# The second and third block of an attention and feed-forward kernel: GpSimd's transfers add half of each group of keys and values, VectorE sums the other half, and the order of all instructions is another

## The chip, the cores and the metric

The kernel runs on one core of one Trainium2 chip. The metric is the device time of one execution in microseconds (us). The core's engines run side by side, each through a queue of its own: TensorE (PE in the views; PEld are its loads of weights), VectorE (DVE), ScalarE (ACT), GpSimd (POOL) and SyncE (SP), which here only issues transfers. A transfer (DMA) is issued by an engine's queue (SPq, POOLq) and done by 16 DMA engines.

## The reference

Two parts, one after the other. Attention over 8 batches and 8 heads, 576 tokens, 64 numbers for each head, in which keys and values are first averaged over groups of eight tokens, so that 576 keys become 72. Then a gated layer over the 4608 tokens with 512 inputs and 1536 hidden numbers.

```python
k_p = k.reshape(B, H, Sp, pool, D).mean(axis=3)      # pool = 8, Sp = 72
v_p = v.reshape(B, H, Sp, pool, D).mean(axis=3)
scores = scale * np.matmul(q, k_p.transpose(0, 1, 3, 2))
scores = scores - np.max(scores, axis=-1, keepdims=True)
attn = np.exp(scores)
attn = attn / (np.sum(attn, axis=-1, keepdims=True) + 1e-09)
return np.matmul(attn, v_p).astype(np.float32)
...
gate = 1.0 / (1.0 + np.exp(-(x @ w_gate)))
val = x @ w_val
return (gate * val @ w_out).astype(np.float32)
```

## The kernel before

The tokens are cut into nine blocks of 512. Block 0 goes alone through the layer, the other eight go in pairs, with sums and differences of blocks and weights that save products. Every large matrix is used as a high and a low half, so a product is three matmuls. The function `first_pass` does attention for blocks 0 to 2 and the whole layer for block 0; after it `attention` does two pairs of heads of a block at a time, beside the products of the pair ahead (`hidden`, `second_sums`).

The host lays keys out as `kT` (for each batch and pair of heads 128 rows, 64 numbers of two heads, by 576 tokens) and values as `vm` (128 rows, the first 64 groups of two heads, by 64 numbers of eight tokens each) and `vr` (the last eight groups). The eight tokens of a group are neighbours, so the sum over a group is a reduction of VectorE over the last axis. `fill` (lines 621 to 637) issues the transfer of a tile and returns this view of it, `pool` (640) sums it. In `first_pass`, `load_k` (1200), `load_v` (1206) and `load_r` (1209) fill tiles for blocks 1 and 2: eight tiles of keys (128x576) and eight of values (128x512), and `keys` (1218) and `v_sum` sum them. For block 0 the keys come the same way, one whole tile for each pair of heads (`h<-in_kT` in the trace), and its values are summed by TensorE from plain rows (`vn`) and a matrix of ones (`sums8`): these are the matmuls `vr` and `vp`. The constants (`const`, tile `cst`: a unit matrix and masks) come in one transfer of 68.5 KB. Sums of keys are put into `kbd`, tiles with two heads on the diagonal, which GpSimd sets to zero first; scores are `sc`. `place_vres` and `v_put` write the values of the last groups into `vres` by a mask, one half for each head.

Some matmuls of the first pass have no reader: `bank_for` issues as many as the table `UNREAD` says ahead of a product, on `kbd` or on the unit matrix in `cst`, into the tile that the product then fills. They appear as `sc<-kbd`, `tr<-cst`, `tp<-cst` and `av<-cst`.

What sets the order: `first_pass` reads the word list `ORDER`, and each word records one step; `Book` takes down every instruction as a unit and nothing is issued. At the end all units are issued in the order of the table `LATER`, 3717 numbers that were found by search. Each engine keeps to its part of that order, and waits in it are for data and for buffers.

Of the kernel before, what the change touches and what calls it, by code (L numbers as in the profile page):

```python
# [19 lines left out]
P = 128  # L20
# [103 lines left out]
6 20 18 9 19 2 26 16 101 25 14 35 21 86 7 24 87 11 29 36 34 0 5 37 4 46 41 27 47 45 88 3 32 31 42 15 30 38 13 75 28 39  # L124
17 83 44 93 56 77 10 57 68 43 52 53 12 23 50 58 78 48 79 54 94 33 61 51 84 81 67 65 59 22 89 82 95 40 102 66 128 74 72
99 73 71 117 64 163 1 132 96 164 124 165 131 137 130 166 126 100 138 134 60 97 151 177 139 62 98 111 121 85 112 135 113
185 114 127 136 152 184 153 122 129 154 125 157 145 173 133 160 182 146 183 156 147 168 123 209 188 192 55 238 148 144
69 149 142 140 141 155 143 76 103 161 159 243 80 104 105 189 116 271 106 187 107 190 191 150 115 108 176 109 201 170
110 202 200 216 171 217 215 167 180 218 169 193 213 158 220 211 197 224 212 225 198 194 70 195 242 174 199 229 344 227
226 205 233 175 208 222 210 206 203 228 204 223 221 277 172 234 214 240 232 181 196 241 207 252 255 235 236 219 260 262  # L130
268 237 256 239 231 265 251 247 162 263 254 253 280 267 279 275 230 304 286 283 289 310 266 257 278 290 269 294 313 272
246 282 179 285 296 245 291 178 287 258 90 288 321 284 322 327 350 292 264 328 281 331 270 332 347 369 244 333 348 312
298 259 346 345 340 302 316 261 91 354 274 276 376 293 305 378 297 309 299 361 92 315 352 355 303 364 250 301 356 320
391 119 365 329 372 366 338 317 379 306 359 308 307 384 383 393 49 395 311 349 439 318 353 362 462 403 324 314 397 339
373 249 408 375 343 351 494 273 248 374 367 326 440 396 394 387 436 385 386 382 368 388 498 370 407 377 447 399 337 406
450 390 454 295 341 458 334 502 319 445 444 118 423 420 342 424 323 425 421 360 507 381 380 466 491 409 449 520 389 410
524 457 435 120 499 426 467 357 468 413 481 427 418 422 485 463 541 433 464 414 434 465 459 441 442 496 484 412 497 438
506 428 508 469 483 510 411 415 448 511 455 475 417 501 523 392 477 443 482 504 489 540 490 542 480 500 509 437 429 543
503 486 532 470 471 460 566 430 431 476 472 473 517 474 495 512 492 300 514 416 515 527 567 522 529 568 521 461 531 325
533 583 576 330 526 516 571 493 537 335 519 525 528 589 544 577 518 534 546 581 586 535 585 539 556 557 595 538 358 548  # L140
553 604 363 608 559 545 530 536 582 550 547 609 551 371 569 560 549 554 570 606 336 555 579 400 627 432 610 561 633 580
634 563 552 565 624 614 564 628 562 404 635 611 629 186 625 588 587 596 584 640 617 603 618 591 638 592 605 575 590 639
572 626 574 558 573 630 724 631 632 594 578 642 647 601 593 649 613 612 615 452 664 730 600 678 620 619 675 607 679 637
621 667 622 676 623 641 598 672 636 668 673 644 597 680 513 479 648 674 398 599 669 488 654 646 689 655 677 401 446 704
602 643 670 671 453 662 698 653 699 657 487 700 659 616 661 731 684 650 683 658 701 666 451 702 660 697 707 713 708 686
709 688 744 703 681 705 687 706 685 694 682 695 651 690 726 725 732 656 711 733 728 691 710 719 717 1034 712 743 692
718 785 714 645 723 746 693 663 720 456 715 665 721 696 716 478 722 749 754 751 736 735 741 734 739 769 738 737 740 770
727 745 747 748 1033 764 753 755 729 774 768 761 756 765 419 779 767 772 742 809 777 807 759 758 757 793 760 773 778
776 780 781 782 783 771 752 784 402 787 775 766 797 811 791 798 801 1035 803 799 1082 806 786 1037 405 788 813 789 804
814 790 850 825 1036 802 652 826 851 822 817 810 853 794 855 827 1263 805 859 856 808 819 1083 818 820 834 843 812 816  # L150
815 831 823 848 844 832 833 824 840 828 841 795 837 838 63 881 821 864 829 894 830 862 912 852 839 871 842 915 792 860
849 865 835 908 872 878 836 916 877 918 882 868 880 869 866 800 867 909 874 879 910 870 899 873 845 900 926 875 846 901
876 911 896 897 941 898 905 902 927 942 854 928 913 903 904 943 906 914 907 886 885 936 1038 847 994 505 884 998 887
930 1039 931 1081 888 932 917 929 861 1040 937 1043 950 893 933 934 1042 935 949 925 892 956 921 923 938 890 957 1084
958 883 1041 891 940 953 922 924 954 939 889 955 1063 895 1265 951 967 1264 1138 944 1064 863 1268 945 1266 1136 1066
1267 963 1137 959 948 962 977 1272 750 974 978 1269 1068 960 965 979 966 952 1271 971 946 857 972 920 1065 973 1067 975
976 1273 1085 1086 988 964 1146 999 968 1344 995 1008 983 1087 1274 1009 996 1089 763 1000 1091 1088 1270 961 997 1090
980 1018 981 1111 1054 1275 1112 1055 1019 1113 1116 1115 982 1010 1002 947 1114 1139 1056 1003 1140 1011 1141 1012 987
1004 1013 8 1147 1016 1014 986 1119 1212 1030 796 1050 1051 990 969 984 1015 1346 993 1345 919 1020 1120 985 1211 1069
1183 1121 1024 762 858 970 989 1347 1025 1348 1026 1131 1017 1132 1021 1353 991 1031 1148 1022 1349 992 1070 1133 1032  # L160
1023 1073 1350 1060 1074 1354 1351 1005 1213 1027 1416 1098 1352 1075 1006 1356 1142 1134 1044 1355 1052 1007 1099 1150
1047 1053 1135 1057 1149 1061 1058 1071 1028 1072 1059 1076 1045 1077 1048 1143 1102 1095 1046 1100 1247 1078 1214 1152
1049 1535 1144 1096 1092 1106 1001 1101 1029 1062 1122 1107 1108 1418 1145 1079 1117 1123 1109 1169 1417 1154 1103 1421
1128 1118 1151 1422 1124 1104 1423 1170 1164 1419 1420 1093 1425 1080 1166 1094 1215 1216 1153 1097 1171 1129 1167 1165
1110 1184 1158 1172 1185 1125 1426 1193 1161 1159 1427 1187 1246 1162 1130 1174 1428 1189 1188 1488 1160 1155 1424 1248
1191 1176 1186 1194 1228 1217 1192 1156 1175 1126 1536 1202 1127 1157 1195 1163 1205 1179 1173 1177 1220 1168 1537 1222
1221 1203 1178 1219 1218 1190 1105 1249 1206 1230 1208 1196 1180 1209 1316 1236 1231 1223 1315 1204 1181 1317 1197 1250
1224 1244 1489 1238 1325 1490 1198 1229 1237 1210 1234 1257 1235 1239 1233 1232 1207 1241 1276 1182 1260 1245 1258 1493
1199 1242 1251 1491 1243 1492 1200 1277 1240 1295 1318 1278 1252 1259 1261 1300 1319 1225 1320 1326 1335 1254 1226 1253
1400 1296 1494 1285 1289 1329 1336 1496 1255 1256 1399 1227 1302 1538 1495 1279 1337 1292 1333 1327 1301 1293 1280 1384  # L170
1290 1294 1281 1282 1283 1303 1262 1284 1201 1357 1297 1497 1304 1334 1305 1298 1498 1328 1572 1299 1321 1360 1306 1286
1291 1307 1287 1378 1361 1338 1310 1385 1308 1389 1311 1401 1331 1380 1379 1312 1451 1394 1358 1404 1499 1313 1339 1397
1500 1314 1405 1370 1391 1395 1340 1322 1390 1461 1396 1323 1288 1366 1309 1363 1403 1359 1448 1574 1364 1573 1429 1406
1575 1402 1407 1381 1408 1462 1362 1410 1409 1398 1324 1330 1577 1432 1392 1341 1332 1449 1433 1438 1342 1382 1393 1434
1515 1452 1377 1479 1365 1516 1411 1576 1442 1430 1412 1413 1578 1581 1501 1371 1580 1376 1463 1414 1450 1443 1445 1477
1517 1415 1431 1446 1372 1466 1478 1447 1439 1444 1373 1582 1539 1454 1467 1480 1584 1374 1649 1502 1504 1579 1540 1375
1583 1481 1383 1533 1505 1437 1440 1343 1518 1544 1435 1436 1464 1603 1519 1468 1525 1441 1455 1545 1546 1465 1367 1482
1456 1566 1503 1534 1453 1520 1459 1469 1457 1552 1549 1547 1460 1458 1470 1368 1483 1585 1507 1369 1484 1550 1601 1548
1650 1591 1551 1652 1508 1471 1567 1602 1386 1509 1472 1387 1526 1473 1476 1632 1553 1506 1604 1475 1474 1586 1595 1653
# [183 lines left out]
def attention_then_ffn(ctx: ExitStack, tc: tile.TileContext, qT, kT, vm, vr, vn, sums8, wgv, wo, const, out, outT):  # L363
# [253 lines left out]
    def slot(b, p):  # L617
        return (b * PAIRS + p) % RING


    def fill(raw, kind, *at):
        if kind == "k":
            nc.sync.dma_start(raw, kT[at])
            return raw.rearrange("p (g t) -> p g t", t=POOL)
# [512 lines left out]
    def first_pass():  # L1137
# [62 lines left out]
        def load_k(j, p):  # L1200
            raws["k", j, p] = fill(raw_room(), "k", j, p)
# [344 lines left out]
```

## Time and profile before

| | |
|---|---|
| median of 3 runs | 876.58 us (876.39 to 876.77) |
| the profiled execution | 876.07 us |
| its span, from first to last instruction | 874.2 us |
| TensorE busy | 865.1 us, 99% of the span |
| TensorE weight loads | 755.9 us, 86% |
| VectorE busy | 684.5 us, 78% |
| ScalarE busy | 540.6 us, 62% |
| GpSimd busy | 24.3 us, 3% |
| granted TensorE clock, mean | 0.999 |
| transfers | 223.11 MB, 255 GB/s over the span |

An engine is busy while it executes an instruction; issuing transfers and waiting are not busy. Times in the views are counted from the start of the span, so the execution's time is the span and some 1.9 us around it.

### The profile page before, as it was taken

The numbers are of one execution on the slowest core, as the hardware profiler recorded it, in microseconds if no ns is written. First come the engines' busy times: TensorE is split into PE (matmuls) and PEld (weight loads), VectorE is DVE, ScalarE is ACT, GpSimd is POOL, SyncE is SP. The second block draws the span as 40 slices with busy tenths as digits, with TensorE's granted clock in tenths as the row PEclk, the third lists the DMA queues.
The fourth block names the chain that finished last, engine by engine and source line by source line (L and its number), as shares of the span: only waits on it lengthen the run. The fifth ranks groups of instructions, "written<-read, shape, count | busy, mean of one in ns | idle before, by whom it ended". The sixth has DMA issues, their size and how long they took to land.

```text
span 874.2 us, 12442 instructions
## 1 busy us (share of the span) xinstructions
PE 865.1 (99%) x4327; PEld 755.9 (86%) x4327; DVE 684.5 (78%) x1067; ACT 540.6 (62%) x981; POOL 24.3 (3%) x60
## 2 busy tenths in 40 slices
PE   8999999999999999999999999999999999999997
PEld 8788888888888888888888888888888888888886
DVE  7999999999999999766779996455588945443973
ACT  7999897688888566565465647433456542233442
POOL 1000000021201000000000000000000000000000
PEclk9999999999999999999999999999999999999999
DMA  9999978999968797787856787666536765766466
GB/s 348 377 334 351 352 255 314 311 339 326 349 254 290 254 318 254 235 278 266 258 198 199 238 293 247 225 205 204 170 119 225 245 195 200 264 199 190 133 206 190
DMA packets 97277, 223.11 MB, mean 255 GB/s; under 512 B 10304, under 2 KB 29248, under 8 KB 95680
## 3 DMA queue, kind: packets, MB, share of 16 engines
q1 hardware_dynamic: 92096, 203.98, 69.3%
q0 software_dynamic: 5120, 18.35, 5.4%
q8 instruction: 34, 0.56, 0.3%
q14 instruction: 27, 0.22, 0.1%
HBM read 168.81 MB, written 53.48 MB: 254 GB/s over the span
## 4 chain that ended last, share of the span: by engine, by line
PE 96%; DMA 1%; DVE 1%; ACT 1%; issue 0%; SPq 0%; DVEq 0%; ACTq 0%
PE chain L333 56%; PE acc L333 28%; PE av L333 4%; PE sc L333 4%; PE tp L333 2%; DMA xs<-in_vn 1%; DMA h<-in_kT 0%; PE vp L333 0%; DVE y L333 0%; PE tr L333 0%; DVE zs L333 0%; ACT L333 0%; SPq L333 0%; DVE h L333 0%; ACT e L333 0%
## 5 line engine op out<-in xcount | busy, mean ns | idle before, releaser
L333 PE MATMUL chain<-xo,parts 128*128 128x512 f32 x2316 | 517.5, 381 | 0.1
L333 PEld LDWEIGHTS chain<-xo,parts 128*128 128x128 f32 x2316 | 433.7, 189 | 61.6 <-DVE y L333 0.7
L333 PE MATMUL acc<-hs,oparts 128*128 128x512 f32 (+1 forms) x1011 | 224.2, 380 | 0.0
L333 PEld LDWEIGHTS acc<-hs,oparts 128*128 128x128 f32 x1011 | 189.3, 189 | 26.4 <-issue 0.2
L333 DVE TENSOR_TENSOR y<-chain,sV 128x512 f32<-128x512 f32 x69 | 46.7, 685 | 49.9 <-PE chain L333 29.6
L333 DVE TENSOR_TENSOR y<-chain,sG 128x512 f32<-128x512 f32 x69 | 46.9, 686 | 43.0 <-PE chain L333 31.1
L333 ACT COPY sG<-chain 128x512 f32<-128x512 f32 x69 | 39.8, 585 | 60.9 <-PE chain L333 60.9
L333 DVE TENSOR_TENSOR hs<-h,hs 128x1024 fp32r<-128x1024 f32 x52 | 63.0, 1219 | 11.5 <-ACT hs L333 11.5
L333 ACT CAST hs<-h 128x1024 fp32r<-128x1024 f32 x52 | 54.5, 1050 | 26.9 <-PE acc L333 26.5
L333 ACT COPY sV<-chain 128x512 f32<-128x512 f32 x69 | 39.8, 584 | 39.4 <-PE chain L333 33.3
L333 ACT ACTIVATE gate<-y 128x512 f32<-128x512 f32 x69 | 43.2, 630 | 32.8 <-DVE y L333 24.4
L333 ACT CAST hs<-s 128x1024 fp32r<-128x1024 f32 x36 | 37.6, 1048 | 30.4 <-DVE s L333 11.8
L333 ACT ACT_TABLE_LOAD x39 | 50.0, 1283 | 3.2 <-DVE y L333 2.6
L333 DVE TENSOR_TENSOR h<-y,gate 128x512 f32<-128x512 f32 x69 | 46.9, 687 | 1.0
L333 DVE TENSOR_TENSOR hs<-s,hs 128x1024 fp32r<-128x1024 f32 x36 | 43.7, 1218 | 4.8 <-ACT hs L333 4.5
L333 PE MATMUL sc<-kbd,raw 128*128 128x144 f32 (+1 forms) x260 | 41.1, 296 | 0.0
L333 PEld LDWEIGHTS sc<-kbd,raw 128*128 128x128 f32 (+1 forms) x260 | 34.0, 178 | 5.2 <-issue 1.4
L333 PE MATMUL acc<-oparts,hs 128*128 128x512 f32 x144 | 38.2, 394 | 0.0
L333 DVE TENSOR_REDUCE m<-sc 128x4 f32<-128x288 f32 x48 | 21.6, 450 | 13.3 <-PE sc L333 13.1
L333 PEld LDWEIGHTS acc<-oparts,hs 128*128 128x128 f32 x144 | 26.7, 189 | 4.1 <-issue 0.2
L333 ACT ACTIVATE gate<-chain 128x512 f32<-128x512 f32 x23 | 13.7, 596 | 25.8 <-PE chain L333 25.6
L333 ACT CAST xo<-s 128x1024 fp32r<-128x1024 f32 x16 | 16.7, 1046 | 18.8 <-DVE s L333 9.9
(202 smaller groups left out, 1028.4 us busy)
## 6 DMA issues: line engine op xcount, KB each, us to landing
oparts<-keptS SPq DMA_DIRECT2D x96, 256.0 KB, 3.7
oparts<-keptO SPq DMA_DIRECT2D x72, 256.0 KB, 4.0
raw<-in_wgv SPq DMA_DIRECT2D x12, 1024.0 KB, 8.2
out<-o SPq DMA_DIRECT2D x35, 256.0 KB, 3.7
raw<-in_kT SPq DMA_DIRECT2D x28, 288.0 KB, 4.4
raw<-in_qT SPq DMA_DIRECT2D x29, 256.0 KB, 4.8
raw_o<-in_wo SPq DMA_DIRECT2D x12, 512.0 KB, 6.2
keptO<-oparts SPq DMA_DIRECT2D x12, 512.0 KB, 4.3
```

Source lines behind the costliest of these rows:

```text
L333: return self._book.take(lambda: f(*args, **named))
```

## The change

The host stores each row of `kT`, `vm` and `vr` in another order (`by_quads`): first the first four tokens of all groups, then the second four. `fill` returns the same data as a view with the halves and the four tokens as two axes (`quads`), and `pool` sums over both (`AX.XY`). For keys and values of blocks 1 and 2 a new function, `fill_added`, is used: SP loads the first half of a row's tokens (128x288 of keys, 128x256 of values), and GpSimd issues a transfer that adds the second half to it on the way (`accum_op`). VectorE then sums four numbers for each group, not eight. The sixteen more instructions are the transfers on GpSimd's queue. `LATER` is replaced as a whole (3733 numbers); `ORDER`, `SECOND`, `UNREAD` and `HOMES` are the same.

```diff
 LATER = """
-6 20 18 9 19 2 26 16 101 25 14 35 21 86 7 24 87 11 29 36 34 0 5 37 4 46 41 27 47 45 88 3 32 31 42 15 30 38 13 75 28 39
...
+4 25 26 6 20 10 18 3 21 2 19 13 29 56 5 24 41 70 91 47 17 92 82 78 32 35 36 98 34 28 57 99 83 42 46 27 106 60 45 37 38
...
+    def quads(raw):
+        return raw.rearrange("p (h n t) -> p n h t", h=2, t=POOL // 2)
+
     def fill(raw, kind, *at):
         if kind == "k":
             nc.sync.dma_start(raw, kT[at])
-            return raw.rearrange("p (g t) -> p g t", t=POOL)
+            return quads(raw)
...
-        return raw.rearrange("p (d t) -> p d t", t=POOL)
+        return quads(raw)
+
+    def fill_added(raw, kind, *at):
+        src, n = (kT[at], S) if kind == "k" else (vm[at], D * POOL)
+        half = raw[:, :n // 2]
+        nc.sync.dma_start(half, src[:, :n // 2])
+        nc.gpsimd.dma_start(half, src[:, n // 2:], accum_op=ALU.add)
+        return half.rearrange("p (n t) -> p n t", t=POOL // 2)
...
     def pool(out, raw, eng):
 
-        if eng is nc.vector:
-            nc.vector.reduce_sum(out=out, in_=raw, axis=AX.X)
-            return
...
+        nc.vector.reduce_sum(out=out, in_=raw, axis=AX.XY if len(raw.shape) == 4 else AX.X)
...
         def load_k(j, p):
-            raws["k", j, p] = fill(raw_room(), "k", j, p)
+            raws["k", j, p] = fill_added(raw_room(), "k", j, p)
...
         def load_v(j, p):
-            raws["v", j, p] = fill(raw_room(), "v", j, p)
+            raws["v", j, p] = fill_added(raw_room(), "v", j, p)
...
         def keys(j, p):
-            k = raws["k", j, p] if j else got[f"k{p}"].rearrange("p (g t) -> p g t", t=POOL)
-            nc.vector.reduce_sum(out=ks[j, p][:, :KEYS], in_=k, axis=AX.X)
+            pool(ks[j, p][:, :KEYS], raws["k", j, p] if j else quads(got[f"k{p}"]), nc.vector)
...
+def by_quads(x):
+    *lead, n, t = x.shape
+    return x.reshape(*lead, n, 2, t // 2).swapaxes(-3, -2).reshape(*lead, n * t)
...
-    kT = k.transpose(0, 1, 3, 2).reshape(B, PAIRS, P, S)
+    kT = by_quads(k.transpose(0, 1, 3, 2).reshape(B, PAIRS, P, KEYS, POOL))
```

The new table moves instructions on every engine. Four places follow. All of an engine's rows are in the order in which it executes them.

The first is TensorE (PE) at the start of the program, its last rows ahead of the matmuls `vr`, which sum the values of block 0, and the rows behind them. `kbd` with a number is a tile for keys; `tr<-cst` and `tp<-cst` are matmuls without a reader. Before:

```order
L333 MATMUL sc<-kbd_92 128x128 x3
L333 MATMUL tr<-cst 128x128
L333 MATMUL sc<-kbd_91,early 128x144 x2
L333 MATMUL tr<-cst 128x128
L333 MATMUL tp<-cst 128x128
L333 MATMUL tr<-cst 128x128
L333 MATMUL vr<-xs_202 96x2x64 x4
L333 MATMUL tp<-cst 128x128 x2
L333 MATMUL tp<-cst,early 128x128 x2
```

and of the change:

```order
L334 MATMUL sc<-kbd_92 128x128 x3
L334 MATMUL sc<-kbd_91,early 128x144 x2
L334 MATMUL vr<-xs_202 96x2x64 x4
L334 MATMUL tp<-cst 128x128 x2
L334 MATMUL tp<-cst,early 128x128
L334 MATMUL tr<-cst 128x128 x4
L334 MATMUL tp<-cst 128x128
```

The four matmuls on `cst` that stood ahead of `vr` stand behind it.

The second is SP, the transfers that it issues first. Of the kernel before:

```order
L333 DMA h<-in_kT 128x576 x2
L333 DMA h<-in_qT 128x512
L333 DMA h<-in_kT 128x576 x2
L333 DMA h<-in_qT 128x512 x2
L333 DMA early<-in_qT 128x512
L333 DMA cst<-in_const 128x137
L333 DMA raw_220<-in_wgv 128x2048
L333 DMA xs_202<-in_sums 128x360
L333 DMA xs_202<-in_vn 64x512
L333 DMA raw_225<-in_wgv 128x2048
```

and of the change:

```order
L334 DMA h<-in_kT 128x576 x4
L334 DMA h<-in_qT 128x512 x2
L334 DMA early<-in_qT 128x512
L334 DMA h<-in_qT 128x512
L334 DMA raw_220<-in_wgv 128x2048
L334 DMA xs_202<-in_sums 128x360
L334 DMA xs_202<-in_vn 64x512
L334 DMA raw<-in_kT 128x288
L334 DMA cst<-in_const 128x137
L334 DMA raw_225<-in_wgv 128x2048
```

All key tiles of block 0 come ahead of the first query, the constants come behind the values `in_vn` of 64x512 and behind the first half tile of keys (128x288).

The third is VectorE (DVE) where it sums that tile of keys (`early<-raw 128x72`) and makes the first low half of x (`xo_252<-av,xo_252`), which the first products of the layer read. `w` and `parts` are weights on their way to two halves, `raw` with a number is a loaded one. Before:

```order
L333 TENSOR_SCALAR w_258<-w_258 128x1024
L333 RECIPROCAL early<-zs 128x16
L333 TENSOR_REDUCE early<-raw 128x72
...
L333 TENSOR_TENSOR parts<-w_234,parts 128x2x256
L333 TENSOR_TENSOR r_246<-rest,r_246 128x4x32
L333 TENSOR_REDUCE early<-raw 128x72
L333 TENSOR_TENSOR parts<-w_234,parts 128x2x256
L333 SCALAR_TENSOR_TENSOR w_258<-w_258,raw_225 128x1024
L333 TENSOR_TENSOR xo_252<-av,xo_252 128x512
```

and of the change:

```order
L334 TENSOR_SCALAR zs<-zs 128x16
L334 TENSOR_REDUCE early<-raw 128x72
L334 RECIPROCAL early<-zs 128x16
L334 TENSOR_TENSOR rest<-early 128x128
L334 TENSOR_TENSOR early<-early 128x512
L334 TENSOR_TENSOR r_246<-rest,r_246 128x4x32
L334 TENSOR_TENSOR early<-early 128x512
L334 TENSOR_SCALAR w_258<-w_258 128x1024
L334 TENSOR_TENSOR parts<-w_234,parts 128x2x256
L334 SCALAR_TENSOR_TENSOR w_258<-w_258,raw_225 128x1024
L334 TENSOR_TENSOR xo_252<-av,xo_252 128x512
L334 TENSOR_TENSOR parts<-w_234,parts 128x2x256
```

A second sum of keys and the second half of the weights' `parts` no longer stand ahead of `xo_252`; the four `vres` subtractions, which stood behind the first sum, now stand ahead of it (they are the rows just above those shown).

The fourth is ScalarE (ACT) some 600 us into the program, with the two halves of the tile `vres4_107`, which a product of attention and values reads. Before, from the first of the two to the second, 26 rows on:

```order
L333 ACTIVATE vres4_107<-vrc_1231,cst_84 96x64
L333 CAST vh4_97<-vs_1249 64x64
L333 ACTIVATE vres3_106<-vrc_1231,cst_84 96x64
L333 CAST xo7_1198<-s_1171 128x1024
L333 COPY sV5_1265<-chain_1264 128x512
L333 ACT_TABLE_LOAD
...
L333 COPY sV6_1334<-chain_1321 128x512
L333 ACTIVATE vres4_107<-vrc_1231,cst_84 96x64
```

and of the change:

```order
L334 CAST vh4_97<-vs_1249 64x64
L334 ACTIVATE vres4_107<-vrc_1231,cst_84 96x64
L334 ACTIVATE vres3_106<-vrc_1231,cst_84 96x64
L334 ACTIVATE vres4_107<-vrc_1231,cst_84 96x64
L334 CAST xo3_1197<-s_1171 128x1024
```

Both halves now stand together. At the end of the program TensorE's last rows were, before, three matmuls of 128x256 into `acc_1729` (the left half), six of 128x512 into `acc_1728` and three of 128x256 into `acc_1729` (the right half); now three of the six stand behind the right half. VectorE copies the right half and then does `o_1762<-acc_1736,sG6_1745`, as before.

## Rows read from the trace of the kernel before

**Rows 1.** TensorE's waits over the whole span: what waited for what, us in total, how often, the longest.

```profile
PE sc L333 <- POOL kbd L333: 1.3, 1, 1.3
PE av L333 <- ACT vres L333: 0.8, 1, 0.8
PE sc L333 <- DVE early L333: 0.5, 1, 0.5
PE vr L333 <- DMA xs<-in_vn: 0.3, 1, 0.3
```

**Rows 2.** Busy time by stretch: the stretch, its length, then busy us and number of instructions of PE, PEld, DVE, ACT and POOL, the granted TensorE clock, the share of the DMA engines and GB/s. The last line is the sum over the span.

```profile
0.00:10.00 10.00, 8.56 (x51) 8.21 (x52) 5.05 (x11) 5.17 (x18) 2.48 (x19) 1.00 0.84 296
10.00:20.00 10.00, 9.15 (x65) 7.94 (x65) 9.93 (x21) 9.91 (x31) 0.00 (x0) 1.00 1.04 396
...
60.00:160.00 100.00, 100.00 (x508) 85.88 (x507) 97.18 (x161) 88.87 (x171) 0.89 (x2) 1.00 0.89 317
...
sum 874.20, PE 865.13 PEld 755.90 DVE 684.49 ACT 540.60 POOL 24.30; mean PE 86.51 PEld 75.59 DVE 68.45 ACT 54.06 POOL 2.43
```

**Rows 3.** Timeline of TensorE near 13 us: start, us, engine, line, operation, out<-in, shape, count, and in brackets the idle time before it and what ended that.

```profile
12.56 0.38 PE L333 MATMUL tr<-cst 128*128 128x128 f32 x2
12.79 0.39 PE L333 MATMUL tp<-cst 128*128 128x128 f32 x2
13.01 0.39 PE L333 MATMUL tr<-cst 128*128 128x128 f32 x2
13.73 1.08 PE L333 MATMUL vr<-xs 64*96 64x128 f32 x8 [0.34 <-DMA xs<-in_vn]
```

**Rows 4.** Transfers: first GpSimd's issue of one in its timeline, then the landing of the two that GpSimd issues (engine, operation, count, KB each, us from issue to landing), then of a tile of keys issued at 12.2 us and of the weights issued from 10 to 36 us with their queue's share of the 16 engines.

```profile
152.23 0.67 POOL L333 DMA_DIRECT2D keptG4A<-parts  x1 [149.21 <-DVE vrc L333]
...
keptG4A<-parts POOLq DMA_DIRECT2D x1, 512.0 KB, 3.9
...
keptG4B<-parts POOLq DMA_DIRECT2D x1, 512.0 KB, 6.7
...
raw<-in_kT SPq DMA_DIRECT2D x1, 288.0 KB, 6.9
...
q1 hardware_dynamic: 3327, 10.15, 101.5%
...
raw<-in_wgv SPq DMA_DIRECT2D x5, 1024.0 KB, 9.4
```

**Rows 5.** VectorE's reductions from 0 to 160 us, grouped by shape: out<-in with their shapes, count, then busy us, mean ns of one, and the idle time before them.

```profile
L333 DVE TENSOR_REDUCE early<-sc 128x4 f32<-128x288 f32 x24 | 10.6, 453 | 0.5 <-PE sc L333 0.3
...
L333 DVE TENSOR_REDUCE early<-raw 128x72 f32<-128x576 f32 x8 | 5.8, 731 | 0.0
...
L333 DVE TENSOR_REDUCE early<-raw 128x64 f32<-128x512 f32 x3 | 2.0, 676 | 0.0
```

**Rows 6.** Timeline of VectorE from 13 to 32 us, with the first, second and third sum of a tile of keys for block 1.

```profile
13.48 0.29 DVE L333 TENSOR_TENSOR rest<-e,early 128x128 f32<-128x128 f32 x1
...
18.77 0.69 DVE L333 TENSOR_SCALAR w<-w 128x1024 f32<-128x1024 f32 x1
19.38 0.25 DVE L333 RECIPROCAL early<-zs 128x16 f32<-128x16 f32 x1
19.54 0.69 DVE L333 TENSOR_REDUCE early<-raw 128x72 f32<-128x576 f32 x1
...
20.86 0.90 DVE L333 TENSOR_TENSOR vres<-vr,vres 32x128 fp32r<-32x128 f32 x4
...
23.41 0.75 DVE L333 TENSOR_REDUCE early<-raw 128x72 f32<-128x576 f32 x1
24.07 0.68 DVE L333 TENSOR_TENSOR parts<-w,parts 128x512 fp32r<-128x512 f32 x1
24.67 1.22 DVE L333 SCALAR_TENSOR_TENSOR w<-w,raw 128x1024 uint32<-128x1024 uint32 x1
...
31.12 0.75 DVE L333 TENSOR_REDUCE early<-raw 128x72 f32<-128x576 f32 x1
```

**Rows 7.** Landing of the constants, issued at 4.49 us, and of the values for `vr`, issued at 6.43 us (KB, us from issue to landing).

```profile
cst<-in_const SPq DMA_DIRECT2D x1, 68.5 KB, 4.8
...
xs<-in_vn SPq DMA_DIRECT2D x1, 128.0 KB, 7.2
```

**Rows 8.** Timelines of TensorE and of ScalarE around 617 us: the matmul that waits, and the two copies into halves of `vres`.

```profile
617.97 0.30 PE L333 MATMUL av<-pr,vres 96*128 96x64 f32 x1 [0.78 <-ACT vres L333]
...
606.31 0.35 ACT L333 ACTIVATE vres<-vrc,cst 96x64 fp32r<-96x64 f32 x1
...
617.57 0.34 ACT L333 ACTIVATE vres<-vrc,cst 96x64 fp32r<-96x64 f32 x1
```

**Rows 9.** The tail: timelines of ScalarE, VectorE and SP's queue, and from the page the group of the matmuls into `acc` (busy us, mean ns).

```profile
868.02 0.59 ACT L333 COPY o<-acc 128x512 f32<-128x512 f32 x1 [0.92 <-PE acc L333]
868.41 0.42 DVE L333 COPY o<-acc 128x256 f32<-128x256 f32 x1 [4.94 <-issue]
868.75 0.68 DVE L333 TENSOR_TENSOR o<-acc,sG 128x512 f32<-128x512 f32 x1
...
869.46 1.80 SPq L333 DMA_DIRECT2D out<-o  x4
...
L333 PE MATMUL acc<-hs,oparts 128*128 128x512 f32 (+1 forms) x1011 | 224.2, 380 | 0.0
```

## What I forecast, and from what

> **What bounds the kernel now.** I read four views in this order. The first is the table of busy time by stretch [rows 2]: TensorE is busy 865.13 of 874.20 us, and 100.00 of 100 us from 60 to 160 us. The second is the list of TensorE's waits [rows 1]: between its first matmul and its last it waits four times, 1.3 + 0.8 + 0.5 + 0.3 = 2.9 us in all. The third and fourth are the timelines around these waits [rows 3, 8] and of the tail [rows 9]. VectorE, whose work the change cuts, is nearly as full as TensorE there (97.18 of 100 us from 60 to 160), but TensorE has no wait for it after the start. So the kernel is bound by what TensorE has to do, and the matmuls are the same ones before and after. What can be gained is the waits and the tail, about 2 us, since the first 1.3 us is a matmul waiting for a zeroed tile, which stays.
>
> **The reductions.** The accumulating transfers halve eight sums of 128x576 and eight of 128x512. A sum of 576 takes 731 ns, of 512 676 ns; one of 288 elements takes 453 ns [rows 5]; that one reads scores and not a loaded tile, but it is the nearest in size. Saved: 8 x (731 − 453) = 2.2 us; for the others 256/288 of 453, 403 ns, is my estimate: 8 x (676 − 403) = 2.2 us. Together 4.4 us of VectorE in the first 160 us, and worth 0 on the path, since TensorE has no wait there to lose: its own queue covers it, 100.00 of 100 us [rows 2]. The sums over two axes (two groups of four) cost nothing more if a sum goes by its elements, as 731 for 576 against 676 for 512 has it; if the second axis cost 0.1 us for each of the few dozen, the same cover hides it. Bounds: 0 and 0.
>
> **The accumulating transfers.** They are sixteen transfers of 144 or 128 KB on GpSimd's queue, each waiting for its first half on SP's. No accumulation is in the trace. The nearest rows are GpSimd's own two, of 512 KB: 0.67 us of issue, 3.9 and 6.7 us to land; a key tile of 288 KB took 6.9 us at the same place in the program, and the five 1 MB weights 9.4 us with the queues at 101.5% [rows 4]. So a second half lands 3.9 (lower) to 9.4 us (upper) after the first. I take what GpSimd's own rows span, 3.9 to 6.7 us.
>
> First use: in SP's new order the first half of the first key tile stands right behind the small tile of values that lands near 13.4 us (below). Another 144 KB at 396 GB/s [rows 2] is 0.37 us, so it lands at about 13.7 and the accumulated tile at 17.6 to 20.4. VectorE summed that tile at 19.54 [rows 6]. Now four small subtractions (0.90 us) go ahead of it, a weight step (0.61 us from its start to the next) and a reciprocal (0.16 us) don't; and the constants land at about 13.9 where VectorE came to them by 13.48, which is 0.4 to 0.5 us. So it asks at about 20.2, and the stall is 0 to 0.2 us. Behind the waiting sum stand the parts of the first weights and the first low half of x, which TensorE's first chain reads. They have a lead: a 576 sum and a subtraction (from 23.41 to 24.67, 1.26 us [rows 6]) no longer stand ahead of that low half, and the first sum is 0.28 us shorter, 1.5 us together. The tightest tile after it is the third of keys: its first half comes 6.1 MB after the first one's in the new order, at 400 GB/s 15 us, so at 28 to 30 us, its sum at 32 to 37. VectorE took it at 31.12 [rows 6]; the constants' 0.5 us and two more weight steps of 0.6 us ahead of it make that near 33. A stall of 0 to 4 us there falls into work that the new table has put after what the first chains need. I take 0 for both.
>
> How GpSimd fares beside a full VectorE is seen at 152 us: 0.67 us of issue where VectorE is 97% busy [rows 2, 4]. The Trainium skill, "DMA: Bandwidth & Descriptors", section "SWDGE vs HWDGE vs iDMA", says that GpSimd writes the descriptors of its transfers into SBUF state from which VectorE's two-port mode locks it out; by that rule these transfers could be held up for as long as VectorE's work lasts, which is one way to the first rival; that row does not show it. The same page, "Anatomy of one DMA", has 2.0 us plus the bytes at 436 GB/s; by it an estimate for 144 KB would be 2.3 us, with no stall at all. The rows are longer than that.
>
> **The start.** Three things move [rows 3, 7]. (a) The constants (68.5 KB) no longer stand ahead of the values' tile whose landing ends the wait at 13.73; at 296 GB/s [rows 2] that is 0.24 us, so the matmuls on it start at 13.5. (b) Four filler matmuls on the constants (two records each in the trace, 0.22 us for the two by the starts 12.56, 12.79, 13.01) stand behind those matmuls and no longer ahead. They filled time in which TensorE would have waited; behind, they are work: 4 x 0.22 = 0.88 us. (c) The first query lands behind all four key tiles and no longer behind two, so first scores come later; the scores are still through by about 12.4, ahead of 13.5, and it costs 0: the wait for the values covers it; without that cover it would cost the two key tiles' 590 KB at 296 GB/s, 2.0 us. The wait of 0.5 us for VectorE goes or stays without effect for the same reason. Sum of the start: +0.88 − 0.24 = +0.64. Bounds: −0.24 (the fillers come to lie in gaps that the new order has between 14 and 29 us) and +1.0 (the tile lands no earlier, and the wait grows a little).
>
> **The wait at 617 us.** A product of attention and values waits 0.78 us for a masked copy on ScalarE at 617.57 [rows 8], which stands in its queue behind a table load and a gate. In the new table both copies of this tile stand ahead of that table load, next to the one that was at 606.31. The wait goes: −0.78; at the lower end the gain is 0, where another one follows at once.
>
> **The tail.** TensorE's last three matmuls were on the right half of one tile; VectorE copies that half at 868.41, then adds the other output at 868.75, and the last four stores are issued from 869.46 [rows 9]. In the new table the half comes three full matmuls earlier (0.22 us each, 224.2 over 1011 [rows 9]: 0.65 us), so copy and addition are through by 868.8; last on TensorE is a full tile, which ScalarE copies in 0.59 us after the end at 868.3, and the stores can go from 868.96: −0.5. Bounds: 0 (their order waits for something else) and −0.65.
>
> **The sum.** +0.64 − 0.78 − 0.5 = −0.64 us. The profiled execution took 876.07 us, so 875.43; it lies 0.51 us under the median of the runs shown, 876.58, and I forecast the median: **875.9 us**. With the bounds of the three terms its own range is 876.58 − 0.24 − 0.78 − 0.65 = 874.9 to 876.58 + 1.0 = 877.6.
>
> **Rivals.** First, slower: accumulated tiles that land late. For it: the queues are at 101.5% when they start, loads take 9.4 us, each accumulation begins when its first half is there, and GpSimd's queue is in order, so that one late half holds up the rest. Against: GpSimd's own rows. At 9.4 us the first tile is there at 23.1, VectorE stalls 2.9 us, less the lead of 1.5, so that TensorE waits 1.4 us before its first chains. The third tile then stalls VectorE by 4.4 to 6.4 us, and gates and weights behind it come up to 3 us late. That gives 875.9 + 1.4 to 4.4, 877.3 to 880.3, with 878.9 as its time. It begins to tell from a landing of 20.2 − 13.7 + 1.5 = 8.0 us. Chance 0.22.
>
> Second, faster: every wait behind the first of [rows 1] goes, and the moved fillers lie in gaps: −0.24 − 0.5 − 0.78 − 0.5 = −2.0, 874.5. For it: VectorE has 4.4 us less to do where it is fullest. Against: the wait for the values is one for a transfer, which VectorE does not hurry, and the fillers have to be done somewhere. Chance 0.18.
>
> Third, no change: the table sorts every engine's work anew, and a wait like that at 617 comes up somewhere else (those of [rows 1] are 0.3 to 1.3 us), so that the gain is eaten: 876.6 to 877.6, at 876.9. Nothing in the trace names its place. Chance 0.14. The forecast keeps 0.46.
>
> **How the numbers follow.** A change of under 0.2% (1.75 us: 874.83 to 878.33) can't be told from none here. The second rival lies under that, and 0.01 of the forecast: faster 0.19. Of the first rival 0.18 lies over it: slower 0.18. The rest is 0.63. The range goes from 874.4, just under the second rival, to 878.8, the middle of the first: 0.11 is left out above and 0.08 below.
>
> **What would show it.** Right: no wait near 617 for the masked copy; a wait for the values' tile near 13 us of 1.2 us or more, whose matmuls start near 13.5; GpSimd's sixteen transfers landing in 4 to 7 us, and no wait of VectorE for them above 1.5 us before 30 us; the right half's copy ahead of TensorE's end. Wrong: TensorE waiting for VectorE between 14 and 45 us with one of GpSimd's transfers behind it, or landings above 8 us (first rival); a wait of TensorE that the old list doesn't have (third); or a granted clock under 1.00 after the longer wait at 13 us, of which my sum has nothing.

## The result: 0.9% slower, and the profile after

The changed kernel takes 884.83 us (median of 4 runs, 883.18 to 886.60), the kernel before 876.67 us beside it: a ratio of 1.0087, with a 95% interval from 1.0070 to 1.0104. My 875.9 us was wrong, the sign too, and 884.8 lies above even the first rival's 877.3 to 880.3 us.

The profiled execution's span is 881.9 us, 7.7 us longer. TensorE's waits after the change, in the columns of [rows 1]:

```profile
PE sc L334 <- ACT kbd L334: 1.9, 1, 1.9
PE sc L334 <- DMA h<-in_qT: 1.6, 1, 1.6
PE sc L334 <- POOL kbd L334: 1.6, 1, 1.6
PE acc L334 <- DMA oparts<-keptS: 0.7, 1, 0.7
PE chain L334 <- ACT sV L334: 0.7, 1, 0.7
PE acc L334 <- DVE hs L334: 0.6, 1, 0.6
PE sc L334 <- ACT e L334: 0.5, 1, 0.5
PE sc L334 <- DVE early L334: 0.4, 1, 0.4
PE tp L334 <- DVE early L334: 0.2, 1, 0.2
```

They sum to 8.2 us, against 2.9 in [rows 1]: 5.3 us. Busy time by stretch, as [rows 2], with one short stretch more:

```profile
10.00:20.00 10.00, 9.35 (x71) 8.24 (x70) 9.84 (x19) 9.72 (x32) 1.25 (x2) 1.00 1.05 381
20.00:30.00 10.00, 8.13 (x40) 5.79 (x39) 6.69 (x17) 6.03 (x15) 2.08 (x4) 0.83 1.04 379
...
60.00:160.00 100.00, 99.27 (x507) 84.42 (x506) 93.92 (x156) 90.02 (x169) 8.02 (x11) 1.00 0.93 322
...
sum 881.90, PE 868.03 PEld 755.51 DVE 682.28 ACT 540.96 POOL 39.30; mean PE 86.80 PEld 75.55 DVE 68.23 ACT 54.10 POOL 3.93
...
26.00:29.00 3.00, 3.00 (x10) 1.73 (x9) 2.43 (x4) 2.26 (x5) 0.03 (x1) 0.50 1.06 380
```

TensorE is busy 2.9 us longer with the same matmuls. Half of the 3.00 us from 26 to 29, 1.5 us, is the clock: there it was granted 0.50, the lower of its two levels (1.2 GHz), after TensorE had stood still. 5.3 + 2.9 is 8.2 us, and the tail gave back some 0.5: the 7.7 us. This says where TensorE's time went; what the adding transfers cost of it, the experiments show.

The loss begins at the first tile of keys. Its adding transfer and the load of weights issued beside it, near 14 us (KB, us to landing):

```profile
raw<-in_wgv SPq DMA_DIRECT2D x1, 1024.0 KB, 9.5
raw<-in_kT POOLq DMA_DIRECT2D x1, 144.0 KB, 9.6
```

VectorE's timeline, where it sums this tile, and further on two tiles of block 2:

```profile
20.96 0.17 DVE L334 TENSOR_SCALAR zs<-zs 128x16 f32<-128x16 f32 x1
23.65 0.45 DVE L334 TENSOR_REDUCE early<-raw 128x72 f32<-128x288 f32 x1 [2.51 <-DMA raw<-in_kT]
...
61.23 0.81 DVE L334 TENSOR_REDUCE early<-raw 128x72 f32<-128x288 f32 x2 [2.04 <-DMA raw<-in_kT]
```

ScalarE copies the first sum into `kbd`, and TensorE's first scores of block 1 read it. ScalarE's row, and TensorE's:

```profile
24.13 0.53 ACT L334 ACTIVATE kbd<-early 64x72 f32<-64x72 f32 x2 [2.63 <-DVE early L334]
...
24.72 0.46 PE L334 MATMUL sc<-kbd,raw 128*64 128x144 f32 x2 [1.87 <-ACT kbd L334]
...
31.54 1.54 PE L334 MATMUL chain<-xo,parts 128*128 128x512 f32 x6
...
63.23 1.99 PE L334 MATMUL acc<-oparts,hs 128*128 128x512 f32 x8 [0.58 <-DVE hs L334]
```

VectorE stands still 2.51 us at 21 us, and 2.04 us more before 61 us for two tiles of keys of block 2. For the first tile I had put 0; the two of block 2 are not in my sum.

### The profile page after: what moved, and what is told of

Read it like the earlier page. It is cut to its first block, busy times and chain, and to the rows that moved or that the text cites. A ratio compares the mean times of both kernels' runs of the same rounds, so it can differ in the third digit from the quotient of the medians.

```text
span 881.9 us, 12472 instructions
## 1 busy us (share of the span) xinstructions
PE 868.0 (98%) x4327; PEld 755.5 (86%) x4327; DVE 682.3 (77%) x1067; ACT 541.0 (61%) x981; POOL 39.3 (4%) x76
## 4 chain that ended last, share of the span: by engine, by line
PE 80%; DVE 7%; ACT 2%; DMA 1%; issue 1%; SPq 0%; DVEq 0%; ACTq 0%
PE chain L334 47%; PE acc L334 25%; PE av L334 3%; PE sc L334 3%; DVE h L334 2%; PE tp L334 2%; DVE hs L334 1%; DVE parts L334 1%; DVE y L334 1%; DMA oparts<-keptS 1%; DMA raws<-in_vr 1%; DVE s L334 1%; ACT L334 0%; DVE pl L334 0%; DVE vs L334 0%
## 5 line engine op out<-in xcount | busy, mean ns | idle before, releaser
L334 PE MATMUL acc<-hs,oparts 128*128 128x512 f32 x1011 | 225.2, 380 | 0.7 <-DMA oparts<-keptS 0.7
L334 DVE TENSOR_TENSOR h<-h 128x256 f32<-128x256 f32 (+2 forms) x39 | 28.1, 724 | 0.2
```

Source lines behind the costliest of these rows:

```text
L334: return self._book.take(lambda: f(*args, **named))
```

## The experiments

All runs of one group were made side by side with the kernel before, whose medians there were 877.02 (the first four runs), 877.14 (the next four) and 877.12 us (the last two).

**No adding transfers, new order.** `e1_whole_tiles`:

```diff
-        nc.sync.dma_start(half, src[:, :n // 2])
-        nc.gpsimd.dma_start(half, src[:, n // 2:], accum_op=ALU.add)
-        return half.rearrange("p (n t) -> p n t", t=POOL // 2)
+        nc.sync.dma_start(raw[:, :n], src)
+        book.take(lambda: None)
+        return quads(raw[:, :n])
```

The empty unit stands in the place of GpSimd's transfer, so that `LATER` still fits.

> The new table and the new layout, but SP loads every tile whole, as before the change, and GpSimd's sixteen adding transfers are gone (VectorE sums eight over two axes). Theory A, the adding transfers alone cost the time, the first stall and what follows from it: 875.5 to 877, no wait of TensorE for the first scores of block 1 and none of the old ones at 617. Theory B, the first stall costs its 4.6 us in the first 36 us and the new order of instructions costs the rest by its own waits (at 63, 211, 234 and near 300 us): 879.5 to 881, with these waits still there.

Measured: 879.26 us, 1.0030 of the kernel before (1.0020 to 1.0040). Against the change's 1.0087 the adding transfers cost 0.57%, 5 us, and the new order costs 0.3%, 2 to 3 us, by itself. Theory B had nearly the amount, though not its parts: of the four later waits, those for `sV` and `e` are still there, those for `hs` and `keptS` are not.

```profile
PE sc L334 <- DMA h<-in_qT: 1.8, 1, 1.8
PE sc L334 <- POOL kbd L334: 1.6, 1, 1.6
PE chain L334 <- ACT sV L334: 0.7, 1, 0.7
PE sc L334 <- ACT e L334: 0.5, 1, 0.5
PE tr L334 <- DVE h L334: 0.5, 1, 0.5
PE sc L334 <- DVE early L334: 0.4, 1, 0.4
PE tp L334 <- DVE early L334: 0.3, 1, 0.3
PE chain L334 <- DVE parts L334: 0.2, 1, 0.2
```

They sum to 6.0 us, 3.1 more than in [rows 1], while TensorE is busy 865.28 us, as before. So the new order's own cost lies in waits; the largest new one, 1.8 us for the first query, stands in part where fillers stood before.

**Adding transfers, old order.** `e2_old_table`: `fill_added`, `quads` and `by_quads` as in the change, and in the old `LATER` each adding transfer right behind its first half.

> The old table with the adding transfers, each put right behind its first half; sums and layout as in the change. Theory A: 882 to 887, about as slow as the change, with VectorE waiting for the first tile of keys near 20 us and TensorE after it. Theory B: the first stall alone, 4 to 5 us over the kernel before, 880 to 882. A third reading, that the new order is what costs and an adding transfer is hidden: 876 to 877.

Measured: 906.04 us, 1.0329 (1.0315 to 1.0344): far beyond what each theory gave. In the old order VectorE waits 18.1 us in all for these tiles of keys alone, the longest 6.9 us for the first, whose adding transfer was issued at 19.5 and landed 7.4 us later. The order of the change had already brought the first half forward (issued at 6.93 us, here at 12.67); in the old order adding costs far more than the change shows.

**Only the first tile whole.** `e3_first_whole`: as `e1`, for `("k", 1, 0)` alone.

> The change, but the first tile of keys (block 1, first pair of heads) comes whole by SP; the other fifteen adding transfers stay. If that one tile's late landing (23.6 us, 9.6 us after its issue) makes the loss and the later waits follow from it: 876 to 878. If the first stall is worth only what it costs in the first 36 us: 880 to 881. If the next tiles' adding transfers are late as well and stall VectorE in its place: 882 to 885.

Measured: 881.56 us, 1.0057 (1.0041 to 1.0074), between the expected cases. The wait at 21 us is gone, and the later one is larger, 3.21 us on VectorE, and now reaches TensorE with 1.75 us, not 0.58:

```profile
58.85 0.81 DVE L334 TENSOR_REDUCE early<-raw 128x72 f32<-128x288 f32 x2 [3.21 <-DMA raw<-in_kT]
...
60.84 1.99 PE L334 MATMUL acc<-oparts,hs 128*128 128x512 f32 x8 [1.75 <-DVE hs L334]
```

In the change the first stall had hidden part of the second: TensorE came to it late.

**The wait filled.** `e4_filled_wait`:

```diff
     def score_matmuls(sc, q, segs, p, hf):
         with book.unit():
+            for _ in range(8 if (len(segs), segs[0][1], p, hf) == (2, 64, 0, 0) else 0):
+                nc.tensor.matmul(sc[:, 0, :P], lhsT=ident, rhs=ident, start=True, stop=True)
```

> The change, with eight matmuls without a reader ahead of the first scores of block 1, where TensorE waits 1.9 us and its granted clock is then 0.50 for about 3.2 us. If the lower clock follows from the wait, it stays at 1.00 there and TensorE wins back about half of 3.2 us: 883.2 against 884.8, seen best in the trace. If the clock falls for another reason, or the stretch is bound by VectorE anyway, the time stays at 884.8.

Measured: 884.72 us (882.44 to 885.75), the same as the change. The clock did follow from the wait: from 26 to 29 us it is 1.00 now. But what TensorE won there it lost at the second stall. Its busy time in both stretches, in the columns of [rows 2]:

```profile
26.00:29.00 3.00, 3.00 (x20) 2.20 (x19) 2.97 (x5) 2.78 (x4) 0.09 (x1) 1.00 1.06 387
...
60.00:70.00 10.00, 6.66 (x23) 5.27 (x22) 8.05 (x14) 5.91 (x10) 1.08 (x2) 0.83 0.74 231
```

and the wait, in the timeline:

```profile
63.92 3.68 PE L334 MATMUL acc<-oparts,hs 128*128 128x512 f32 x8 [3.34 <-DVE hs L334]
```

So up to 64 us the transfers bound the kernel through VectorE, and nothing of the 1.5 us of the clock was won. But behind the longer wait the clock is lower instead, 0.83 from 60 to 70 us, and the eight matmuls behind the wait take 3.68 us, 1.99 in the change. What the lower clock costs by itself, this run doesn't show.

**A copy in place of the addition.** `e5_no_add`:

```diff
-        nc.gpsimd.dma_start(half, src[:, n // 2:], accum_op=ALU.add)
+        nc.gpsimd.dma_start(half, src[:, n // 2:])
```

> The change with GpSimd's sixteen second halves as plain transfers over the first halves, not added (this leaves out the second four tokens in the place of the first, so half of each group of keys and values is missing from blocks 1 and 2). Order, bytes and waits are the same. If the adding itself is what makes the tiles late, the first one lands within 4 to 6 us of its issue and the time falls to 879 to 881. If the time lies in the wait for the first half and in the queue of loads that stands ahead of the second, a plain one lands after 9 to 10 us as well: 884 to 885.

Measured: 877.93 us, 1.0018 (1.0007 to 1.0029). It is the addition: with the same bytes, order and waits the first tile lands 5.4 us after its issue and not 9.6, none of the eight tiles of keys of blocks 1 and 2 keeps VectorE waiting, and 0.7%, some 6 us, are won, more than I expected. What is left over the kernel before is 0.6 to 2.5 us. What differs is in the queues' part of the two profiles, from 10 to 125 us, in which all sixteen transfers lie (packets, MB, share of the 16 engines; q1 is SP's, q0 GpSimd's). First the change, then this run:

```profile
q1 hardware_dynamic: 11367, 35.45, 85.2%
q0 software_dynamic: 2304, 2.23, 13.0%
```

```profile
q1 hardware_dynamic: 12048, 37.29, 88.0%
q0 software_dynamic: 768, 2.23, 6.1%
...
raw<-in_wgv SPq DMA_DIRECT2D x1, 1024.0 KB, 8.9
raw<-in_kT POOLq DMA_DIRECT2D x1, 144.0 KB, 5.4
```

The same 2.23 MB go in 144 packets for each transfer and not in 48, and hold the engines for 13.0% of 115 us and not 6.1%: 0.93 us of all sixteen for a tile and not 0.44. The last two rows are the transfers near 14 us: the plain one lands long before the load of weights beside it, the adding one landed with it. How 0.5 us more of the engines makes a landing 4.2 us later isn't shown; in the median of the eight key tiles it is 5.4 us in the change and 4.7 us here.

**Three tiles whole.** `e6_three_whole`: as `e3`, with `("k", 2, 3)` and `("k", 2, 1)` too.

> The change with three tiles of keys whole by SP: the first, for which VectorE waited 2.5 us near 21 us, and the two for which it waited 2.0 to 4.6 us before 61 us. Theory: these waits are all that the adding transfers cost; then 878.5 to 879.5, as with all sixteen whole (879.26). If the stall moves on to other tiles: 881 or more, as with one whole (881.56).

Measured: 879.20 us, 1.0028 (1.0016 to 1.0040), as with all sixteen whole. The other thirteen adding transfers cost nothing that can be told. These three tiles carry the price.

**First halves earlier.** `e7_early_halves`: all sixteen adding transfers; in `LATER` the first tile's first half ahead of the first weights, that of `("k", 2, 3)` ahead of one 1 MB load, and GpSimd's two transfers for block 2 swapped.

> The change with all sixteen adding transfers, but the first halves of those tiles are issued earlier: the first one ahead of the first 1 MB of weights, one of the two near 61 us ahead of a 1 MB load, and GpSimd takes the other of them first. If lateness is the cause, VectorE's waits for these tiles shrink below 1 us and the time falls to 879 to 881; the first values land some 0.4 us later. If an adding transfer is slow or slows others wherever it stands: 883 to 885.

Measured: 880.64 us, 1.0043 (1.0027 to 1.0058). The first tile now lands at 17.8 us, VectorE takes it at 21.89 without a wait, and no tile of the first pass with an adding transfer makes it wait. Lateness was the cause, and it can be moved. What is left over `e1`, 1.4 us, is about the size of two new waits, for the values and the weights that the earlier halves pushed back:

```profile
PE vr L339 <- DMA xs<-in_vn: 0.8, 1, 0.8
PE chain L339 <- DVE parts L339: 0.7, 1, 0.7
```

**The two gains alone, in the old order.** `e8_old_wait_tail` is the kernel before with seven units of `LATER` moved, and no transfer or sum changed.

> The kernel before (its transfers, sums and table) with two places of its order moved: the second masked copy into the tile that TensorE waits for at 617 us stands next to the first, and at the end TensorE does the right half three matmuls earlier, VectorE does the last addition ahead of the copy of that half, and each store is issued as soon as its data are there. If these two terms of my sum were sized right, the wait of 0.78 us goes, and the tail gets shorter by 0.5 us from the matmuls and by up to 1.0 more from the stores: 874.3 to 875.4 against 876.6 to 877. If a wait like it follows elsewhere, or the tail is bound by the last store's landing alone: 876 to 876.6.

Measured: 875.23 us, 0.9982 (0.9974 to 0.9991). The wait at 617 stayed at 0.78 us, now at 619.91. I had moved the copies into `vres4_107`, the tile whose rows stand in the part on the change, and it isn't the one that waits. All that was won is the tail.

`e9_wait_tail` moves the second copy into `vres1_104<-vrc_1289` in its stead.

> As the run with the old table and a new tail, but the masked copy that is moved is now the one that TensorE really waits for at 617 us: its trace kept that wait, because the two copies of the tile that I had named belong to an earlier product; those of the waiting one are the halves with a table load and a gate between them in ScalarE's rows. If that is the wait, it goes and 0.8 us more is won: 874.0 to 874.8 against 876.6 to 877.1 of the kernel before. If it only moves on: 875.2, as without it.

Measured: 874.58 us, 0.9970 (0.9959 to 0.9982): faster than both kernels. That wait is gone, but its trace has another of the same size right behind it:

```profile
619.36 1.56 PE L339 MATMUL chain<-xo,parts 128*128 128x512 f32 x6 [0.84 <-DVE y L339]
...
865.68 2.85 PE L339 MATMUL acc<-hs,oparts 128*128 128x512 f32 x15
...
867.25 2.31 SPq L339 DMA_DIRECT2D out<-o  x5
867.99 0.42 DVE L339 COPY o<-acc 128x256 f32<-128x256 f32 x1 [1.88 <-PE acc L339]
868.57 0.58 ACT L339 COPY o<-acc 128x512 f32<-128x512 f32 x1 [1.34 <-PE acc L339]
```

From 600 to 640 us TensorE is busy 39.16 us, in `e8` 39.11. So the wait moved on, whatever the median says; the two runs' intervals overlap. The gain is the tail: SP's five last stores follow each other from 867.25 without waiting for the last addition, and the span ends at 872.6 us and not at 874.2, though TensorE ends no earlier (865.68 + 2.85 = 868.5).

`e10_values_first`: `e9`, with the sums' matrix and the small tile of values ahead of the first weights.

> The same, and SP issues the sums' matrix and the values for TensorE's first sum of values ahead of the first 1 MB of weights, so that they land some 2.5 us earlier and the weights 0.8 us later. If TensorE's wait of 0.3 us near 13 us is the values' alone: 0.2 to 0.4 us less than the run beside it. If the weights' later landing holds up VectorE and the first products: 0.3 to 1 us more.

Measured: 875.07 us, 0.9972 (0.9961 to 0.9983): no difference from `e9`. The wait for the values is gone from its list; what it was worth can't be told here. The profiled execution is the longest of the seven (877.50 us) and has a wait of 2.0 us for `kbd` up to 7.6 us, which `e9`'s trace doesn't have.

## Why the prediction was wrong

**The step that failed** is that I priced an accumulating transfer like a plain one and then put its stalls at 0. I had the bounds, 3.9 to 9.4 us, and chose what GpSimd's own plain rows span, 3.9 to 6.7 us. For a plain transfer that was right: in `e5` the first tile lands after 5.4 us, with the weights beside it at 8.9. The adding one took 9.6 us. That my upper bound, the weights' 9.4 us [rows 4], comes near it is luck, not a price for adding, which no row before could give; the median of the eight key tiles, 5.4 us, lies within the range that I took. So "I take 0 for both" failed where it counted: VectorE stood still 2.51 us for the first tile and 2.04 us for the two of block 2, and the adding transfers cost 5 us (`e1`) to 6 us (`e5`).

The path was wrong too. I followed the late sum to TensorE's first chain, where the order had a lead of 1.5 us. That chain starts at 31.54 us without a wait. What waited, 1.87 us at 24.72, are the scores that read this tile's own sum through `kbd`; the lead doesn't help them.

By the Trainium skill, "DMA: Bandwidth & Descriptors", "Anatomy of one DMA", an estimate for these bytes is 2.3 us; the first tile's landing in the trace is four times that. That VectorE locks GpSimd out (the Trainium skill, "DMA: Bandwidth & Descriptors", "SWDGE vs HWDGE vs iDMA") is shown by no run here. `e5` doesn't exclude it: VectorE is busy as long there, 682.13 us and 682.28 in the change, but GpSimd's issue of the first tile is shorter as well, 0.68 us and not 1.03.

**The first rival** was right that tiles land late and in VectorE's first place, and too cheap. It had VectorE's first stall at 2.9 us (2.5) and TensorE's wait at 1.4 us (1.87), though ahead of the first chains; it had the third tile as the second place, where nothing waited, and didn't have the two tiles of block 2 near 61 us: the first half of one lands 8.7 us after its issue, GpSimd's queue holds the other's addition behind it until 52.15 us, and that lands after 9.1 us more. Nor did it have the new order's own cost, which it shares with the third rival.

**The third rival** came true in its mechanism, not in its time: in `e1`, `e5`, `e6` and `e7` TensorE waits 0.7 us for `sV` and 0.5 us for `e`, which the list before doesn't have. They belong to the new table, and my sum has nothing for them. I had given this rival 0.14 as if it excluded the first; both held.

**The reductions** were sized right: 445 ns where I had 453, 393 to 411 where I had 403, and a sum over two axes of the same 576 elements takes 753 ns against 751:

```profile
L334 DVE TENSOR_REDUCE early<-raw 128x72 f32<-128x288 f32 x8 | 3.5, 445 | 4.6 <-DMA raw<-in_kT 4.6
L334 DVE TENSOR_REDUCE early<-h 128x72 f32<-128x576 f32 x4 | 2.9, 753 | 3.9 <-DMA h<-in_kT 3.9
...
L334 DVE TENSOR_REDUCE early<-raw 128x64 f32<-128x256 f32 x3 | 1.2, 393 | 0.0
```

That their 4.4 us are worth 0 isn't contradicted: `e5`, with sums of four, is 1.3 us below `e1`, with sums of eight, but the intervals overlap.

**The start** came near in its sum, by luck: the wait was another. `vr` starts at 13.68 us, as at 13.73 before [rows 3], with 0.88 us of fillers left for later, so up to there the loss is some 0.8 us where I had 0.64; in the change the wait up to 24.72 us comes behind it, and how much of the loss reaches the end isn't shown. The long wait ahead of `vr` that I had named isn't there:

```profile
7.69 2.20 PE L334 MATMUL sc<-kbd,h 128*128 128x144 f32 x16 [1.63 <-DMA h<-in_qT]
...
13.68 1.08 PE L334 MATMUL vr<-xs 64*96 64x128 f32 x8
```

The late first query, which I had costed at 0, takes the place of the fillers: TensorE stands still until 7.69 us and reaches `vr` just after the values have landed.

**The wait at 617 us** is gone in the change, as forecast, but I had read it off the wrong rows (`e8`): the halves that belong to 617.57 are those of `vres1_104`. In the change no other wait follows there; in the old order one does (`e9`), which the lower end of my bounds, 0, had foreseen.

**The tail** was right: TensorE ends at 873.79 + 2.64 = 876.43 us and the four stores follow 0.65 us behind it; before, it ended at 859.72 + 8.60 = 868.32 us and the stores came at 869.46 [rows 9], 1.15 us behind. That is −0.5, as I had it. TensorE's row of before, then the rows of the change:

```profile
859.72 8.60 PE L333 MATMUL acc<-hs,oparts 128*128 128x512 f32 x42
```

```profile
873.79 2.64 PE L334 MATMUL acc<-hs,oparts 128*128 128x512 f32 x14
...
875.87 0.43 DVE L334 COPY o<-acc 128x256 f32<-128x256 f32 x1 [4.97 <-PE acc L334]
876.21 0.68 DVE L334 TENSOR_TENSOR o<-acc,sG 128x512 f32<-128x512 f32 x1
...
877.08 1.81 SPq L334 DMA_DIRECT2D out<-o  x4
```

**What stays open.** Why an addition goes in three times the packets, and how that makes one tile land 4.2 us later; how the new table's 2 to 3 us divide among its waits; and where TensorE's other 1.4 us of longer busy time come from, which `e1` doesn't have.

## What to carry to other kernels

Where a kind of transfer is new, the rows of other kinds don't price it, neither those of its queue nor those of its neighbours: a plain transfer in the same place landed after 5.4 us, the adding one after 9.6. If a wait hangs on it, its upper bound belongs into the sum, and the wait is looked for at the first instruction that reads its data. In a kernel that its TensorE bounds at 99%, relief of another engine had almost nothing to win here, and a new dependency (two landings in a row ahead of a sum) had several microseconds to lose. A wait that is to vanish is tied to its instruction by the rows around it, and the sure gain may lie elsewhere: here in when the last five stores go.

## What the runs showed of the hardware

- An adding transfer of GpSimd of 128 or 144 KB goes in 144 packets and takes 0.93 us of all 16 engines; a plain one of the same bytes goes in 48 and takes 0.44 us.
- After TensorE had stood still for 1.87 us up to 24.7 us, its granted clock was 0.50 from 26 to 29 us. With matmuls without a reader in that wait it stayed at 1.00 there; TensorE then stood still for 3.34 us up to 63.9 us, its clock was 0.83 from 60 to 70 us, and the kernel took the same time.
- The first tile's adding transfer landed 9.6 us after its issue, a plain one in its place 5.4 us.
- A sum over two axes costs as much as one over a single axis of the same elements: 753 and 751 ns for 128x576.
